# Asking for two transfers later in a fused attention and mixture-of-experts kernel

## Chip, cores and metric

The kernel runs on one core of a Trainium2 chip. The metric is the time on the device in microseconds.

## The reference

The first half is attention with one key and value head for all query heads: 8 batches, 16 heads, 384 tokens, head size 64. The second half sends each of the 3072 tokens (width 1024, the 16 heads side by side) to one of 16 experts by a gate of two levels and multiplies the expert's output by the two gate weights.

```python
scores = scale * np.matmul(q, k.transpose(0, 1, 3, 2))
scores = scores - np.max(scores, axis=-1, keepdims=True)
attn = np.exp(scores)
attn = attn / (np.sum(attn, axis=-1, keepdims=True) + 1e-09)
x = np.matmul(attn, v)              # then (B, H, S, D) -> (B*S, H*D)
...
g_idx = np.argmax(x @ w_group, axis=1)             # one of 4 groups
e_idx = np.argmax(xg @ w_expert[g], axis=1)        # one of 4 experts in it
h = np.maximum(xg[mask_e] @ w1[g, e], 0.0)
out[tok_idx] = (g_w * e_w)[:, None] * (h @ w2[g, e])
```

## The kernel before

Attention is a loop of 96 steps (`i`). Twelve steps are one batch (a "group" below), in three tiles `t` of 128 tokens with four steps each; a step handles two units of two heads by two. In a step PE makes the scores (L210), DVE their row maxima (L221) and the transposition of the probabilities of two steps before (L245), ACT the exponentials (L224), DVE the reciprocal of the sums (L235), and POOL the scaling (L239). In the first two steps of a tile PE works on the expert of an earlier batch (`main_expert`, L483 and L499) and on the gate's logits (L284); in the last two it multiplies the previous tile's probabilities by the values (`pv`, L261, 96 matmuls each).

At the end of a tile `pv_out` copies the result to `xt` and POOL casts it into `xb` (L276), the batch's tokens in bf16; there are two such buffers. The batch's most frequent expert is computed in place from `xb`. Tokens of other experts are handled after the main work by a loop over a list of (batch, expert) pairs with a count that the gate gives; that loop reads the tokens again from device memory. For this `keep_xb` (L474) copies `xb` of each batch but the last to `xb_scratch`, 768 KB in one DMA. In the profiled execution this loop has no turn.

The order of the work is written out by hand. `at(slot, where, fn, ...)` enters a call in a table, and the loop runs the table's calls of step `i` at fixed places in the step; "g" is the last of them. Each engine, SP included, works its own list of instructions in the order in which the program issues them, and waits only for the data, buffers and earlier transfers that an instruction needs.

SP's list holds, per group: the loads of queries `load_q` (L123, four DMAs of 224 KB for tiles from the sixth on; two buffers, so tile t + 2 takes that of tile t), of keys `load_k` (L133) and values `load_v` (L166, two buffers), the stores of the expert's rows y (L550), and the copy `keep_xb`. POOL issues the loads of the experts' weights (L458). The queries of a tile are reordered by DVE in two halves (`q_blocks`, L199): the first half in the second step of the tile before, the second half in the first step of the tile itself.

At the end of step 16 after the start of a batch, which is the fifth step of the next one, the table before holds the copy, the values' load and the queries' load, in this order.

Of the kernel before, what the change touches and what calls it, by code (L numbers as in the profile page):

```python
# [19 lines left out]
def kernel(  # L20
# [18 lines left out]
    ST = S // P  # L39
# [720 lines left out]
    def at(slot, where, fn, *args):  # L760
        later.setdefault((slot, where), []).append((fn, args))
# [8 lines left out]
    for b in range(B):  # L770
        s0 = SB * b
        for x, j0, j1 in ((s0 + 8, 0, 1), (s0 + 16, 1, ST)):
            at(x, "m2", logits, b, j0, j1)
            at(x + 1, "m0" if b and j0 == 0 else "v", logits_out, b, j0, j1)
        at(s0 + 9, "m0" if b else "v", gate_first, b)
        at(s0 + 9, "m3" if b else "m2", gate_choose, b)
        at(s0 + 9, "w", gate_score, b)
        at(s0 + 9, "w", gate_pick, b)
        at(s0 + (13 if b == B - 1 else 12), "w", gate_picked, b)
        if b == B - 1:  # L780
            at(s0 + 9, "w", load_main, b, 0)
            at(s0 + 10, "w", load_main, b, 1)
        else:
            at(s0 + 9, "g", load_main, b, 0)
            at(s0 + 9, "g", load_main, b, 1)
            at(s0 + 16, "g", keep_xb, b)
        at(s0 + 17, "v", gate_masks, b)
        x = s0 + 18
        at(x, "e", gate_values, b)
        at(s0 + (19 if b == B - 2 else 22), "w", gate_selected, b)  # L790
        if b == B - 1:
            at(s0 + 13, "w", gate_pick_second, b)
        if b + 1 < B:
            at(s0 + 2, "g", load_k, b + 1)
            at(s0 + 4, "g", load_v, b + 1)
            at(s0 + 7, "g", scale_k, b + 1)
            at(s0 + 8, "e", k_blocks, b + 1)
    for t in range(NT):
        for x, u, half in ((4 * t, t, 1), (4 * t + 1, t + 1, 0)):
            if u < TQ:  # L800
                at(x, "m1", q_group, u, half)
            elif u < NT:
                at(x, "e", q_blocks, u, half)
        if t < NT - 2:
            at(4 * t, "g", load_q, t + 2)

    load_k_first()
    load_q(0, first=True)
# [24 lines left out]
    for i in range(NSL):  # L833
        t, p = i // 4, i % 4
# [31 lines left out]
    b = B - 1  # L866
# [137 lines left out]
```

## Time and profile before

| what | value |
|---|---|
| median of 3 runs | 507.35 us (505.65 to 508.06) |
| profiled execution, its own time | 507.63 us |
| span of its instructions | 506.2 us |
| mean granted TensorE clock | 0.992 |
| PE, DVE, ACT, POOL busy | 94%, 82%, 63%, 58% of the span |
| moved by DMA | 83.17 MB, mean 164 GB/s |

Times in the profile are microseconds from the start of the span. In a group's line come the line of the kernel, engine, operation, output and inputs, shapes and count; in a wait's line the one that waits, what released it, then total time, how often, and the longest. An SP row of the timeline is an instruction that issues a DMA, not the transfer itself; "to landing" is the time from issue until the data is there. "PEld" is the loading of matmul weights, "issue" a time in which an engine waited for nothing that the profile shows.

### The profile page before, as it was taken

The page shows a single profiled execution, that of the slowest core. Times are in us where ns is not written, and L with a number is a line of the kernel's source. Part 1 is how long each engine was busy: PE and PEld are TensorE (multiplying, and loading weights), DVE is VectorE, ACT ScalarE, POOL GpSimd, SP SyncE. Part 2 cuts the span into 40 slices and gives each one's busy share as a digit, 9 for nine tenths or more (in the row PEclk, how much of TensorE's full clock was granted, in tenths as well). Part 3 has the DMA queues.
Part 4 walks back from the last instruction along what each step waited for, and adds up shares of the span by engine and source line. Part 5 has one row for each costly group of instructions (what it writes and reads, how often), then busy time and mean ns, then how long its engine had stood idle before and what let it go on. Part 6 is the DMA issues. An engine that isn't in the chain of part 4 may idle for free. (4 is left out here: it accounts for less than half of the span.)

```text
span 506.2 us, 20018 instructions
## 1 busy us (share of the span) xinstructions
PE 478.0 (94%) x8240; PEld 258.8 (51%) x8257; DVE 413.2 (82%) x743; ACT 319.5 (63%) x998; POOL 292.5 (58%) x532
## 2 busy tenths in 40 slices
PE   7597789999999999999999999999999999999993
PEld 3144355555455455554555455554555455555652
DVE  3889979998799888998799988998899888892550
ACT  4776756766765775766766766666666766662420
POOL 1665865585476654585466664774566754675132
PEclk9998999999999999999999999999999999999998
DMA  7612997389955999379964999379964995069993
GB/s 116 130 31 43 172 239 197 74 138 229 246 124 101 209 243 243 71 136 227 239 147 82 203 237 254 73 137 225 224 184 78 192 240 165 3 110 225 245 220 123
DMA packets 63388, 83.17 MB, mean 164 GB/s; under 512 B 20151, under 2 KB 39739, under 8 KB 63040
## 3 DMA queue, kind: packets, MB, share of 16 engines
q0 software_dynamic: 18736, 39.32, 41.9%
q1 hardware_dynamic: 43600, 42.25, 34.0%
q8 instruction: 66, 1.08, 0.9%
q10 hardware_dynamic: 960, 0.30, 0.3%
q14 instruction: 26, 0.21, 0.1%
HBM read 101.52 MB, written 18.22 MB: 237 GB/s over the span
## 5 line engine op out<-in xcount | busy, mean ns | idle before, releaser
L239 POOL TENSOR_SCALAR pr<-pr,rinv 128x384 f32<-128x384 f32 x384 | 217.3, 585 | 149.1 <-DVE rinv L235 136.1
L224 ACT ACTIVATE pr<-s,nmx 128x384 f32<-128x384 f32 x384 | 217.6, 579 | 133.2 <-DVE nmx L221 122.6
L221 DVE TENSOR_REDUCE nmx<-s 128x2 f32<-128x768 f32 x192 | 174.3, 948 | 47.5 <-PE s L210 46.4
L245 DVE STREAM_TRANSPOSE ring<-pr 128x768 f32<-128x768 f32 x192 | 175.4, 952 | 0.1
L210 PE MATMUL s<-kt,qt 64*64 64x384 f32 x1536 | 149.9, 500 | 13.7 <-ACT pr L224 12.4
L261 PE MATMUL x<-ring,v_sb 32*64 32x256 f32 x4608 | 138.4, 379 | 0.1
L261 PEld LDWEIGHTS x<-ring,v_sb 32*64 32x64 f32 x4608 | 101.9, 131 | 43.8 <-issue 23.6
L210 PEld LDWEIGHTS s<-kt,qt 64*64 64x64 f32 x1536 | 48.9, 133 | 82.9 <-ACT pr L224 43.7
L224 ACT ACTIVATION_READ_ACCUMULATOR pr<-s,nmx 128x1 f32 x384 | 77.9, 203 | 0.0
L483 PE MATMUL x<-xb,w 128*128 128x384 bf16 x448 | 76.6, 326 | 0.0
L483 PEld LDWEIGHTS <-w 128*128 128x128 bf16 x512 | 47.7, 98 | 42.2 <-issue 12.6
L499 PE MATMUL x<-w,h_t 128*128 128x512 bf16 x276 | 64.6, 380 | 0.6
L499 PEld LDWEIGHTS <-h_t 128*128 128x128 bf16 x392 | 36.4, 98 | 51.5 <-issue 12.1
L458 POOL DMA_DIRECT2D w<-in_moe_w_dram x36 | 27.4, 772 | 10.8 <-issue 8.9
L275 ACT COPY xt<-x 128x256 f32<-128x256 f32 x96 | 28.9, 387 | 3.1 <-PE x L261 3.1
L489 ACT ACTIVATE h_t<-x 128x384 bf16<-128x384 f32 x56 | 25.3, 501 | 6.5 <-PE x L483 6.5
L518 ACT ACTIVATE y<-x,gsel 128x512 f32<-128x512 f32 x36 | 24.8, 693 | 3.2 <-PE x L499 3.2
L276 POOL CAST xb<-xt 128x1024 bf16<-128x1024 f32 x24 | 24.9, 1036 | 3.2 <-ACT xt L275 3.2
L199 DVE STREAM_TRANSPOSE qt<-q_sb 128x512 f32<-128x512 f32 x38 | 26.1, 688 | 0.0
L499 PE MATMUL sb<-w,h_t 128*128 128x512 bf16 (+1 forms) x99 | 21.5, 362 | 0.3
L518 ACT ACTIVATE y<-sb,gsel 128x512 f32<-128x512 f32 (+1 forms) x10 | 6.7, 666 | 18.6 <-PE sb L499 18.6
L235 DVE RECIPROCAL rinv<-ssum 128x4 f32<-128x4 f32 x96 | 13.9, 145 | 3.2 <-ACT pr L224 3.2
(134 smaller groups left out, 157.4 us busy)
## 6 DMA issues: line engine op xcount, KB each, us to landing
w<-in_moe_w_dram POOLq DMA_DIRECT2D x36, 1024.0 KB, 13.2
q_sb<-in_q_dram SPq DMA_DIRECT2D x76, 224.0 KB, 6.0
out_dram<-y SPq DMA_DIRECT2D x84, 128.0 KB, 6.6
xb_scratch<-xb SPq DMA_DIRECT2D x7, 768.0 KB, 4.3
v_sb<-in_v_dram SPq DMA_DIRECT2D x32, 96.0 KB, 3.9
kk<-in_k_dram SPq DMA_DIRECT2D x28, 92.0 KB, 3.9
q_sb<-in_q_dram SPq DMA_DIRECT2D x16, 128.0 KB, 3.4
q_sb<-in_q_dram SPq DMA_DIRECT2D x5, 64.0 KB, 3.0
```

The source lines that it names most:

```text
L199: nc.vector.transpose(out=qt[:].rearrange("p (x d) -> p x d", d=32), in_=q_sb[:, :, 0:32])
L210: nc.tensor.matmul(out=s[m * D:(m + 1) * D, h, 0:S], lhsT=qt[r, ts(2 * cc + m, D)], rhs=kt[r, :], start=True, stop=True, tile_position=(h ...
L221: nc.vector.tensor_reduce(out=nmx[:], in_=s[:, :, 0:S], axis=AX.X, op=ALU.max, negate=True)
L224: nc.scalar.activation(out=pr[:, h, :], in_=s[:, h, 0:S], func=ACTF.Exp, bias=nmx[:, h:h + 1], scale=1.0, accum_out=ssum[:, k, h:h + 1],)
L239: nc.gpsimd.tensor_scalar(out=pr, in0=pr, scalar1=rinv[:, k, h:h + 1], scalar2=1.0, op0=ALU.mult, op1=ALU.mult)
L245: nc.vector.transpose(out=ring[:, (u // 4) % 3, u % 4].rearrange("p h s -> p (h s)"), in_=st.pop(("pr", u))[:].rearrange("p h s -> p (h s)"),)
L261: nc.tensor.matmul(out=o[i][h * D:(h + 1) * D, 0:2 * P].rearrange("d (g c q) -> d g c q", g=2, c=4), lhsT=v_sb[r, n, :], rhs=ring[r, a:z + ...
L275: nc.scalar.copy(out=xt[:, :, ts(i, 32)], in_=o[:, 0:2 * P].rearrange("p (c q) -> p c q", c=KO))
L458: nc.gpsimd.dma_start(out=w[:, o:o + 4, :], in_=views[n][ds(e, 1), :, o:o + 4, :].rearrange("o p c f -> (o p) c f"))
L483: nc.tensor.matmul(out=hp[:, 0:S], lhsT=w1[:, ko, ts(fc, P)], rhs=xb[:, ko, :], start=(ko == 0), stop=(ko == KO - 1))
L499: nc.tensor.matmul(out=yp, lhsT=h_t[:, fo, ts(j, P)], rhs=w2[:, fo, at_:at_ + w], start=(fo == 0), stop=(fo == FO - 1),)
L518: nc.scalar.activation(out=y[:, at_:at_ + w], in_=yp, func=ACTF.Copy, scale=g)
```

## The change

The copy of the tokens is entered at the end of step `s0 + 19` in place of `s0 + 16` (`s0` is the batch's first step; seven copies). For tiles with `t > 3` and `t % 3 == 1` the load of the queries of tile `t + 2` is entered at the end of step `4 * t + 2` in place of `4 * t`; these are six loads. No instruction is added or removed.

```diff
         else:
             at(s0 + 9, "g", load_main, b, 0)
             at(s0 + 9, "g", load_main, b, 1)
-            at(s0 + 16, "g", keep_xb, b)
+            at(s0 + 19, "g", keep_xb, b)
         at(s0 + 17, "v", gate_masks, b)
...
         if t < NT - 2:
-            at(4 * t, "g", load_q, t + 2)
+            at(4 * t + (2 if t > ST and t % ST == 1 else 0), "g", load_q, t + 2)
```

## The prediction

> **What bounds the kernel now.** I read the page first, then the waits of the engines, then the waits and the timeline of SP (the queue that the change edits), and last PE in the steps around the copy.
>
> ```profile
> span 506.2 us, 20018 instructions
> ...
> PE 478.0 (94%) x8240; PEld 258.8 (51%) x8257; DVE 413.2 (82%) x743; ACT 319.5 (63%) x998; POOL 292.5 (58%) x532
> ...
> q8 instruction: 66, 1.08, 0.9%
> ```
>
> PE is busy for 94% of the span. The third line counts the packets that bring instructions: 66 of them with 1.08 MB, so about 16 KB each; they matter for one rival below. The waits of the engines say who holds whom:
>
> ```profile
> POOL pr L239 <- DVE rinv L235: 136.1, 78, 9.7
> ACT pr L224 <- DVE nmx L221: 122.6, 88, 3.7
> DVE nmx L221 <- PE s L210: 46.4, 60, 2.4
> PEld s L210 <- ACT pr L224: 43.7, 79, 2.3
> ...
> PEld x L261 <- issue: 23.6, 42, 0.6
> ...
> PEld x L187 <- DMA wge<-in_moe_w_expert_dram: 0.6, 1, 0.6
> ```
>
> PE, DVE and ACT hold one another in the softmax loop. In the whole answer one line alone names a transfer for which a computing engine waits: 0.6 us for the gate's weights, once, at the start. No engine waits for queries, values or the tokens' copy. So a step of attention ends by PE and the softmax chain, not by a transfer, and what the change can win is not a wait for data. It moves transfers on SP, and SP's own waits are these:
>
> ```profile
> SPq L550 <- ACT y L518: 152.0, 10, 34.4
> SPq L123 <- DVE qt L199: 71.9, 9, 14.2
> SPq L133 <- DMA q_sb<-in_q_dram: 43.3, 20, 4.3
> ...
> SPq L474 <- POOL xb L276: 12.0, 1, 12.0
> ```
>
> SP works its list in order and mostly stands at a store of y, at a q buffer that is not yet free, or at a k load that wants earlier q loads landed. The slots of the program ("step 16", "step 18") are therefore only places in that list, not times.
>
> **Which time the copy and the q load have.** The timeline of SP in the third group of twelve steps (the last row is from a narrower window and shows the third and fourth DMA of the first q load):
>
> ```profile
> 184.24 7.46 SPq L133 DMA_DIRECT2D kk<-in_k_dram  x4
> 191.80 1.77 SPq L550 DMA_DIRECT2D out_dram<-y  x4
> 193.67 0.38 SPq L474 DMA_DIRECT2D xb_scratch<-xb  x1
> 194.14 2.63 SPq L166 DMA_DIRECT2D v_sb<-in_v_dram  x4
> 196.87 15.62 SPq L123 DMA_DIRECT2D q_sb<-in_q_dram  x8
> ...
> 197.77 0.94 SPq L123 DMA_DIRECT2D q_sb<-in_q_dram  x2
> ```
>
> And DVE, where each step has one reciprocal (L235) and the two reorderings of queries (L199) per tile:
>
> ```profile
> 188.94 0.14 DVE L235 RECIPROCAL rinv<-ssum 128x4 f32<-128x4 f32 x1
> 188.99 0.68 DVE L199 STREAM_TRANSPOSE qt<-q_sb 128x512 f32<-128x512 f32 x1
> ...
> 196.41 0.14 DVE L235 RECIPROCAL rinv<-ssum 128x4 f32<-128x4 f32 x1
> ...
> 204.66 0.14 DVE L235 RECIPROCAL rinv<-ssum 128x4 f32<-128x4 f32 x1
> ...
> 209.33 0.14 DVE L235 RECIPROCAL rinv<-ssum 128x4 f32<-128x4 f32 x1
> ...
> 210.00 0.67 DVE L199 STREAM_TRANSPOSE qt<-q_sb 128x512 f32<-128x512 f32 x1
> ...
> 215.69 0.71 DVE L199 STREAM_TRANSPOSE qt<-q_sb 128x512 f32<-128x512 f32 x1
> ```
>
> The reciprocals at 188.94, 196.41, 204.66 and 209.33 are those of steps 16, 17, 19 and 20 of the group. The q load of "step 16" needs the buffer that L199 finishes reading at 188.99 + 0.68 = 189.67. SP comes to it at 196.87, over 7 us after it is free, because it first has k, y, the copy and v to issue. So SP never waits there for step 16, and would not wait for step 18 either.
>
> **The change part by part.**
>
> *The q load put two steps later* (six loads of four DMAs). SP's list from step 16 to 20 reads y, copy, v, q, q before, and y, v, q, copy, q after. Nothing that SP waits for stands between step 16 and step 18 of the list, and the q load keeps the one condition that it had, the buffer free at 189.67. So it isn't asked for later: without the copy ahead of it, it is asked for 194.14 - 193.67 = 0.47 us earlier, at 196.4, and v at 193.7. It is first used at 215.69, about 19 us after. Price: 0. What hides it is that distance:
>
> ```profile
> L474 SPq DMA_DIRECT2D xb_scratch<-xb x7: 370/376/386, 76.0 to 422.8; - x7
> DMA to landing us min/median/max: 3.7/4.3/5.1
> ...
> DMA to landing us min/median/max: 3.0/6.0/17.2
> ```
>
> The first two lines are the copy's, the last that of the q loads of L123: at their longest, 17.2 us, a load asked for at 196.4 lands at 213.6, still before 215.69. With the cover gone DVE would stand at L199, and the next row maxima (L221) and through them ACT and PE behind it.
>
> *The copy put three steps later* (seven copies; six change places with v and q, the seventh has neither near it). It is now issued after v (2.73 us from 194.14 to 196.87) and q (197.77 + 0.94 - 196.87 = 1.84 us): 193.67 + 2.73 + 1.84 = 198.2, some 4.6 us later, in step 18 and not in step 19. Nobody reads what it writes within the timeline, and its source buffer is one of two, written again a whole group of twelve steps later. Behind it on SP stands only the second q load, which can't start before L199 ends at 210.00 + 0.67 = 210.67. Price: 0; it would cost something only if the copy took until then, over 12 us against 5.1 at most. In the first group the copy also waited 12.0 us for POOL's cast (the line of SP's waits), with v and q behind it; v need no longer stand behind that wait, and no engine waits for v. Price: 0.
>
> *What the transfers then look like.* The windows show the burst and the empty stretch (the columns end with PEclk, DMA share and GB/s):
>
> ```profile
> 193.70:198.00 4.30, 4.30 (x55) 2.19 (x61) 4.16 (x11) 2.59 (x9) 1.63 (x4) 1.00 0.97 316
> 198.00:203.50 5.50, 5.50 (x158) 3.47 (x150) 5.33 (x9) 3.63 (x13) 3.58 (x8) 1.00 0.99 188
> 203.50:210.50 7.00, 7.00 (x162) 3.96 (x150) 5.93 (x10) 5.40 (x18) 5.26 (x11) 1.00 0.03 7
> ```
>
> The engines that move data are full from 193.7 to 203.5 and empty from 203.5 to 210.5. The change issues the same DMAs, all by 198.6, so the burst keeps its length and the empty stretch stays empty; only the order inside changes, q ahead of the copy.
>
> *What PE sees of the order.* The one trace of transfers on PE that I find is in the product with the values (L261), step 19 of a group; five groups, PE's rows, and of the second the rows of the weight loads:
>
> ```profile
> 144.47 2.85 PE L261 MATMUL x<-ring,v_sb 32*64 32x256 f32 x96
> ...
> 201.68 3.29 PE L261 MATMUL x<-ring,v_sb 32*64 32x256 f32 x96
> ...
> 259.34 3.23 PE L261 MATMUL x<-ring,v_sb 32*64 32x256 f32 x96
> ...
> 316.93 3.18 PE L261 MATMUL x<-ring,v_sb 32*64 32x256 f32 x96
> ...
> 374.47 2.85 PE L261 MATMUL x<-ring,v_sb 32*64 32x256 f32 x96
> ...
> 201.68 0.62 PEld L261 LDWEIGHTS x<-ring,v_sb 32*64 32x64 f32 x18 [0.60 <-issue]
> 202.56 1.96 PEld L261 LDWEIGHTS x<-ring,v_sb 32*64 32x64 f32 x78 [0.26 <-issue]
> ```
>
> The same 96 matmuls take 2.85 us in two groups and 0.44, 0.38 and 0.33 us longer in three. Nothing releases PE there ("issue"): its list of instructions stops for a moment after the 18th weight load, while q is arriving. I read it as a block of instructions that came late among the data packets; this is inferred. In all it is 0.44 + 0.38 + 0.33 = 1.15 us. Putting the copy behind q can remove it (lower bound -1.15 us) or give one such stop to each of the seven copies (upper bound 7 x 0.44 = +3.1 us). I take 0: at 201.7 the engines that move data are full before and after.
>
> The Trainium skill ("Runtime: NRT & Kernel Launch", Instruction fetch mechanics) says that instructions come in blocks of 16 KiB over a DMA queue of their own, fetched while the engine runs the previous ones, and mostly hidden. The size agrees with the packets of the page; the 0.26 us gap is not hidden, if my reading is right. By the page the term is 0, as taken.
>
> Sum: 0 + 0 + 0 on the profiled execution's 507.63 us (span 506.2 and 1.43 around it). That one lies 0.28 us above the median of the three runs, so the forecast is the median, rounded: 507.4 us. The runs went from 505.65 to 508.06 without any change.
>
> **The rivals.** *The stops go away.* If the data packets beside q were what delayed the instructions, the three stops vanish: 507.35 - 1.15 = 506.2 us. For it: they occur only in the steps in which the burst lies. Against it: the burst is as full as before. This is still within 0.5%.
>
> *Every copy brings a stop (slower).* Place: steps 18 to 20 of a group. The copy, now at 198.2 and behind q in the queue, moves to about 201 to 204, into PE's densest lists, the product with the values at 201.68 and what follows. If each of seven copies makes PE stop once for 0.44 us, the time is 507.35 + 3.1 = 510.4 us. It decides for slower from 2.54 / 7 = 0.36 us per group. For it: three of five groups show a stop of that size now. Against it: two groups with the same burst show none, and scores and experts' matmuls leave PE's list more room than L261 does. The Trainium skill ("DMA: Bandwidth & Descriptors", Queues, rings and completion order) says that a data engine turns between queues a whole packet at a time; by that rule large packets ahead of a block of instructions hold it up longer, and this rival follows. No row here separates packets of one size from those of another.
>
> *It does what it says.* If the list does bind SP to the steps, q is asked for before the reciprocal of step 19 at 204.66 and the copy after it, at some 205 to 207, into the empty stretch. The burst gets shorter, q still lands ahead of 215.69 at its median of 6.0 us (asked for at 204, at 210), and the time is that of the first rival at best, 506.2 to 507.4 us. Against it: SP issued k, y, copy, v and q back to back.
>
> **How the numbers follow.** A measurement of this kernel can tell about 0.5%, 2.54 us, from no change. Forecast 507.4 us: 0.64. Stops gone, 506.2: 0.16. A stop per copy, 510.4: 0.13. As it says: 0.07. The range reaches from 505.3 (the lowest run is 505.65; two cases lean to that side) to 509.9 us, below the price of the slower rival, whose chance is most of what is left out. Faster by over 0.5% needs a gain of which no row shows the source, and gets 0.12 for that, from the tails of the forecast and of the two cases below it; slower gets 0.10 from the copy's rival and 0.05 from tails, 0.15; within 0.5% the rest, 0.73.
>
> **What would show it.** Right: on SP's timeline y, v, q, copy back to back, v about half a microsecond earlier, the copy 4 to 5 us later, near 198; the stretch from 203.5 to 210.5 as empty as before; no new line of a computing engine waiting for a transfer. Wrong, towards the slower rival: L261 of step 19 over 3 us in more groups than three, with gaps put down to "issue". Wrong in the premise: the copy issued after 204, or L199 waiting for a q load.

## The result and the profile after

Over 20 runs of each the change has a median of 508.49 us (505.28 to 509.66) and the kernel before 505.76 us (504.31 to 508.06). The ratio is 1.0047, 95% interval 1.0033 to 1.0061: 0.47% slower, 2.4 us by the ratio. That is within the 0.5% of the forecast's class, but the interval reaches past it. The three runs known ahead lay high; the median before is 1.6 us lower than they said. The profiled execution took 507.77 us with a span of 506.3. All ratios here leave out runs more than 1.5% above the fastest of their kernel: two of twelve in experiment 3 (704 us at a granted clock of 0.655, which stays unexplained), five of twelve in 5 and one of six in 12.

SP's timeline of the third group after:

```profile
191.03 1.77 SPq L550 DMA_DIRECT2D out_dram<-y  x4
192.90 1.76 SPq L166 DMA_DIRECT2D v_sb<-in_v_dram  x4
194.77 1.85 SPq L123 DMA_DIRECT2D q_sb<-in_q_dram  x4
196.72 0.40 SPq L474 DMA_DIRECT2D xb_scratch<-xb  x1
210.47 1.79 SPq L123 DMA_DIRECT2D q_sb<-in_q_dram  x4
```

The order is y, v, q, copy, q, back to back. Counted from the first store of y, v is asked for 0.47 us earlier than before (1.87 for 2.34), q 1.33 us earlier (3.74 for 5.07) and the copy 3.8 us later (5.69 for 1.87). Nothing comes two or three steps later. The windows, moved by the 0.8 us that this execution is ahead (columns as before, the last two DMA share and GB/s):

```profile
192.90:197.20 4.30, 4.30 (x54) 2.23 (x60) 4.20 (x10) 2.52 (x9) 1.78 (x4) 1.00 0.83 233
197.20:202.70 5.50, 4.98 (x130) 2.87 (x122) 5.32 (x9) 3.71 (x13) 3.52 (x9) 1.00 0.98 248
202.70:209.70 7.00, 7.00 (x178) 4.21 (x166) 5.21 (x9) 5.17 (x18) 4.65 (x9) 1.00 0.03 11
```

The first window is less full than before (0.83 for 0.97), the burst ends where it ended, and the empty stretch is as empty as before (0.03). What is new is in the second line: PE is busy for 4.98 of 5.50 us, where it was busy for all. The product with the values in step 19 shows where, group by group (PE's rows; where it stopped in the middle, two rows with the gap behind the second):

```profile
85.46 0.86 PE L261 MATMUL x<-ring,v_sb 32*64 32x256 f32 x17
86.74 2.42 PE L261 MATMUL x<-ring,v_sb 32*64 32x256 f32 x79 [0.42 <-issue]
...
143.52 2.85 PE L261 MATMUL x<-ring,v_sb 32*64 32x256 f32 x96
...
200.73 1.07 PE L261 MATMUL x<-ring,v_sb 32*64 32x256 f32 x18
202.33 2.41 PE L261 MATMUL x<-ring,v_sb 32*64 32x256 f32 x78 [0.52 <-issue]
...
259.10 2.85 PE L261 MATMUL x<-ring,v_sb 32*64 32x256 f32 x96
...
316.31 1.07 PE L261 MATMUL x<-ring,v_sb 32*64 32x256 f32 x19
317.67 2.41 PE L261 MATMUL x<-ring,v_sb 32*64 32x256 f32 x77 [0.29 <-issue]
...
374.45 2.85 PE L261 MATMUL x<-ring,v_sb 32*64 32x256 f32 x96
```

The third group took 202.33 + 2.41 - 200.73 = 4.01 us for what takes 2.85 without a stop. In the three groups that stop, PE loses 0.85, 1.16 and 0.92 us (from the first weight load to the last, against 2.26 us without a stop), 2.93 us in all; before it was 1.15 us. The line of the waits that holds these stops, that of L261, went from 23.6 to 25.6 us in total and from 0.6 to 1.0 us for the longest; the line of L210 hardly moved (26.9 us before):

```profile
PEld s L210 <- issue: 27.3, 151, 1.2
PEld x L261 <- issue: 25.6, 42, 1.0
```

No computing engine has a new wait for a transfer. The steps say the same, each taken from one reciprocal of DVE (L235) to the next: from step 24 of the loop to its end no step differs by more than 0.03 us between the two profiles, except step 19 of the third, fourth and fifth group (+0.72, -0.38 and +0.59 us), which are the stops. The two spans are nearly equal (506.2 and 506.3) because the profiled execution of before lost about as much in its first 24 steps; single profiles show where time is lost, the ratio says how much on average.

### The profile page after: what moved, and what is told of

Its sections match the earlier page's. It is cut to its first block, busy times and chain, and to the rows that moved or that the text cites. A ratio compares the mean times of both kernels' runs of the same rounds, so it can differ in the third digit from the quotient of the medians.

```text
span 506.3 us, 20018 instructions
## 1 busy us (share of the span) xinstructions
PE 477.1 (94%) x8240; PEld 257.4 (51%) x8257; DVE 412.9 (82%) x743; ACT 319.9 (63%) x998; POOL 293.6 (58%) x532
## 3 DMA queue, kind: packets, MB, share of 16 engines
q8 instruction: 66, 1.08, 0.9%
## 5 line engine op out<-in xcount | busy, mean ns | idle before, releaser
L210 PE MATMUL s<-kt,qt 64*64 64x384 f32 x1536 | 149.1, 497 | 13.5 <-ACT pr L224 12.4
L261 PE MATMUL x<-ring,v_sb 32*64 32x256 f32 x4608 | 138.9, 379 | 1.4 <-issue 1.2
L261 PEld LDWEIGHTS x<-ring,v_sb 32*64 32x64 f32 x4608 | 101.4, 131 | 45.6 <-issue 25.6
L210 PEld LDWEIGHTS s<-kt,qt 64*64 64x64 f32 x1536 | 48.4, 132 | 83.1 <-ACT pr L224 44.0
L235 DVE RECIPROCAL rinv<-ssum 128x4 f32<-128x4 f32 x96 | 13.9, 144 | 3.3 <-ACT pr L224 3.3
```

What stands on the lines that cost most here:

```text
L210: nc.tensor.matmul(out=s[m * D:(m + 1) * D, h, 0:S], lhsT=qt[r, ts(2 * cc + m, D)], rhs=kt[r, :], start=True, stop=True, tile_position=(h ...
L261: nc.tensor.matmul(out=o[i][h * D:(h + 1) * D, 0:2 * P].rearrange("d (g c q) -> d g c q", g=2, c=4), lhsT=v_sb[r, n, :], rhs=ring[r, a:z + ...
```

## The experiments

Ratios are to the kernel before, run on the same chip beside each, with 95% intervals.

**1. The queries' part alone.**

```diff
             at(s0 + 16, "g", keep_xb, b)
...
-            at(4 * t, "g", load_q, t + 2)
+            at(4 * t + (2 if t > ST and t % ST == 1 else 0), "g", load_q, t + 2)
```

> Only the queries' line of the change; the copy stays at step 16. If my reading of SP holds (the step of the program is only a place in SP's list, and nothing lies between the two places), this is before's list of instructions on every engine and the ratio to before is 1.000 within its interval, some 0.1 to 0.2%. If putting the load two steps later counts by itself, the ratio is near the whole change's 1.005 and SP issues the load later than before, near 205 us in the third group.

Measured 0.9991 (0.9975 to 1.0007). The list of instructions is that of before on every engine, SP included: this part of the change is nothing. It also shows how a kernel without any change varies: its trace has one stop of 0.11 us in step 19 of all groups, before's had three of 0.33 to 0.44.

```profile
PEld x L261 <- issue: 22.9, 39, 0.6
```

The whole change is therefore one of order: v and q ahead of the copy. Is it the copy behind q that costs, or q being earlier?

**2. No copy.**

```diff
-            at(s0 + 19, "g", keep_xb, b)
```

> The change without the seven copies (their scratch stays unwritten; the loop that would read it has no turn). Theory A, the copy's data behind q holds up a block of PE's instructions: the stops of L261 in step 19 fall to at most before's (1.15 us in all, against some 2.9 us after), ratio 0.995 to 1.000. Theory B, it is v and q being asked for about half a microsecond to two microseconds earlier that puts q onto the block of instructions: they are as early here, so stops of 0.9 to 1.2 us stay and the ratio is 1.004 to 1.006.

Measured 1.0013 (0.9993 to 1.0034), between the two theories. Stops stay in three groups (1.05, 0.67 and 0.38 us), but the mean is nearer to before than to the change.

```profile
PEld x L261 <- issue: 24.5, 42, 0.9
```

So the copy behind q is a good part of the cost (1.0047 against 1.0013). PE still stops here without any copy, but so it does before, and a ratio of 1.0013 can't be told from 1.

**3. The copy held to step 19.**

```diff
+    def hold(b):
+        nc.sync.dma_start(out=mark_dram[b], in_=st["rinv"][0:16, 0, 0:1])
...
+            at(s0 + 19, "g", hold, b)
             at(s0 + 19, "g", keep_xb, b)
```

> The change, with a 64-byte store of the reciprocals of step 19 ahead of each copy on SP, so that the copy can't be issued before that step: now it is asked for near 205 us in the third group, in the stretch without transfers, as the change's words have it. Theory A: no copy data meets the block of instructions that step 19 needs, stops at most before's, ratio 0.995 to 1.000, faster than the change by 0.5 to 1%. Theory B: as the change, 1.004 to 1.006.

Measured 1.0012 (0.9991 to 1.0032), the same as with no copy at all, though above what theory A gave. The copy was now really in the empty stretch, some 9 us behind q:

```profile
193.97 1.85 SPq L124 DMA_DIRECT2D q_sb<-in_q_dram  x4
202.93 0.32 SPq L476 DMA_DIRECT2D mark<-rinv  x1
203.34 0.74 SPq L479 DMA_DIRECT2D xb_scratch<-xb  x1
```

Two ways of taking the copy out of the burst give one result. Neither ratio can be told from 1, so they don't show that q being earlier costs something by itself.

**4. The copy in small rows.**

```diff
-    xb_dram = nc.dram_tensor("xb_scratch", [B, P, KO * S], BF16).ap()
+    xb_dram = nc.dram_tensor("xb_scratch", [B, P, KO, S + 32], BF16).ap()
...
-        nc.sync.dma_start(out=xb_dram[b], in_=st["xb", b][:].rearrange("p c t -> p (c t)"))
+        nc.sync.dma_start(out=xb_dram[b][:, :, 0:S], in_=st["xb", b][:])
```

> The change, with the copy's rows in the scratch padded, so that it moves pieces of 768 bytes in place of 6144 (the same bytes, eight times the packets). If it is the size of the copy's packets that holds up the instructions: stops back to before's, ratio 0.998 to 1.002. If it is only that the data engines are full for longer at this point: the copy takes longer than before (about 3 us at the rate of q), stops stay or grow, ratio 1.004 to 1.010.

Measured 1.003 (1.0003 to 1.0057): it reaches into both expectations. In its profile the instruction packet that comes between steps 18 and 19 took at most 1.29 us in any of the six groups, against 2.50 us in one group of the change. With one profile of each, whether large packets hold up the instructions more than small ones still stays open.

**5. The copy twice.**

```diff
     def keep_xb(b):
+        if b < B - 1:
+            nc.sync.dma_start(out=xb_again[b], in_=st["xb", b][:].rearrange("p c t -> p (c t)"))
         nc.sync.dma_start(out=xb_dram[b], in_=st["xb", b][:].rearrange("p c t -> p (c t)"))
```

> The change, with each copy made twice in a row (the second into a scratch of its own). If the copy's data behind q is what makes PE's block of instructions late, a burst longer by one more copy (some 2.5 to 3 us) finds the block more often: more or longer stops in step 19, ratio to before 1.006 to 1.012. If only the order of v and q counts, or if the block is caught by q alone, nothing is added: 1.003 to 1.006, as the change.

Measured 1.004 (1.0003 to 1.0077), below the figure expected and inside the other case's 1.003 to 1.006. But the twelve runs spread from 505.08 to 517.18 us, and their median is 511.67 against 506.80 us, 1.0096. The profile is of a run of 508.21 us; PE stops in step 19 of five of the six groups there, 3.1 us in all, against three groups and 2.93 us in the change. What the longest runs lost isn't shown by a profile, so I count this as support, not proof.

**6. Both transfers really later.** POOL reads a column of the old queries at step 18, so SP has to wait for that step before it loads into the buffer.

```diff
+    def still_read(t):
+        touch = pool.tile([P, 1], FP32, tag="touch", bufs=1)
+        nc.gpsimd.tensor_copy(out=touch[:], in_=st["q", t][:, 0, 0:1])
...
+        if t > ST and t % ST == 1 and t < NT - 2:
+            at(4 * t + 2, "g", still_read, t)
         if t < NT - 2:
             at(4 * t + (2 if t > ST and t % ST == 1 else 0), "g", load_q, t + 2)
```

> The change, with one read of a column of the old queries by POOL at step 18 (six reads), so that SP has to wait for step 18 before it loads into that buffer, and the copy behind it on SP comes later still: now both transfers come when the change's words say, q near 204 and the copy near 206 in the third group. Theory A, the block of instructions that PE needs in step 19 (asked for near 198 to 200) is late because of q and the copy: at that time the data engines are nearly empty, so step 19 has no stops, and the ratio is 0.994 to 0.998. Rival, stops have nothing to do with transfers: they stay as in the change, 1.003 to 1.006. Rival, the next block (near 204) is caught in its place and stops appear in step 20: 1.000 to 1.004.

Measured 0.998 (0.9959 to 1.0001), 0.67% below the change. SP's timeline and PE's line of waits (L265 is L261 of the other kernels):

```profile
194.45 1.77 SPq L170 DMA_DIRECT2D v_sb<-in_v_dram  x4
204.77 1.80 SPq L123 DMA_DIRECT2D q_sb<-in_q_dram  x4
206.62 0.45 SPq L478 DMA_DIRECT2D xb_scratch<-xb  x1
210.61 1.79 SPq L123 DMA_DIRECT2D q_sb<-in_q_dram  x4
```

```profile
PEld x L265 <- issue: 22.9, 39, 0.6
```

Step 19 has no stop in any group, and none came up in step 20. This is what the change's words describe, and it isn't slower.

**9. Only the queries really later.** The same read by POOL, with the copy at its old place ahead of v (`at(s0 + 16, "g", keep_xb, b)`).

> The kernel before, its copy at its old place ahead of v, and only the queries of every third tile made to wait for step 18 by POOL's read. Compared with the version in which q and the copy both come late. If q is what catches the block of instructions between steps 18 and 19 (stops stayed without any copy), this alone removes the stops of step 19: ratio 0.995 to 1.000, like that version's 0.998. If the copy has to be out of the way too, the ratio stays at 1.000 to 1.003 with stops in step 19.

Measured 0.9984 (0.9965 to 1.0003), as in 6, and again no stop in step 19. SP's timeline, then PE's line of waits:

```profile
191.64 0.37 SPq L478 DMA_DIRECT2D xb_scratch<-xb  x1
192.11 2.62 SPq L170 DMA_DIRECT2D v_sb<-in_v_dram  x4
202.65 8.08 SPq L123 DMA_DIRECT2D q_sb<-in_q_dram  x8
```

```profile
PEld x L265 <- issue: 23.2, 40, 0.6
```

The copy may stay where it was. In this profile it is enough that q is not under way between steps 18 and 19; the ratio alone, whose interval reaches 1.0003, doesn't show a gain over before.

**7 and 8. Other beginnings of the blocks.** In the profile before there are 66 instruction packets of 16 KB to PE's 8240 matmuls and 8257 weight loads, some 250 to a packet; what one packet brings is called a block here. 128 instructions more for PE, about half a block, in the change (7) and in the kernel before (8):

```diff
-    busy(5)
+    x = xbank()
+    for _ in range(69):
+        nc.tensor.matmul(out=x[:, 0:32], lhsT=blank[:, 0:P], rhs=blank[:, 0:32], start=True, stop=True)
     prep_first()
```

> The change, with 69 matmuls of 32 columns in place of the 5 of 512 that warm PE up at the start: 128 more instructions, half a block of 16 KB, so every later block of PE's list begins half a block earlier in the program; transfers and data as in the change; at most 1 us is added at the start. If the stops come from blocks that are fetched between steps 18 and 19, where q and the copy are under way, they go or move to other steps, and with the dense list of L261 no longer at the end of a late block the ratio to before is 0.994 to 1.001. If the transfers disturb PE in another way (its reads or writes of SBUF), the shift changes nothing: stops in step 19, 1.004 to 1.007.

> The kernel before with the same 128 instructions more at the start. By the theory of late blocks its stops in step 19 (1.15 us in the profile) go as well, and with them the difference between the two orders on SP: ratio 0.994 to 1.000, and within 0.2% of the change shifted in the same way. If the transfers disturb PE in another way: 1.000 to 1.002.

Measured 1.0274 (1.0242 to 1.0306) and 1.02 (1.017 to 1.023). The gain didn't come. In both profiles nearly all stops left step 19 (two remain in 7) and came up in steps 15 to 17 of each of the seven later groups, about 2 us a group. PE's rows of step 15 in the fourth group of 7:

```profile
240.44 1.52 PE L210 MATMUL s<-kt,qt 64*64 64x384 f32 x16
241.89 1.98 PE L261 MATMUL x<-ring,v_sb 32*64 32x256 f32 x64
244.47 1.12 PE L261 MATMUL x<-ring,v_sb 32*64 32x256 f32 x32 [0.59 <-issue]
```

That settles what the stops are. The work and the transfers of 8 are those of before and only the place in the program where each 16 KB begins was moved, and the time rose by 2%. In the traces of all fourteen kernels the weight loads of L261 stop 45 times for 0.2 us or more, and each time they go on 1.19 to 1.57 us after the end of an instruction packet. The packets ahead of L261's stops in step 15 took only 0.96 to 1.01 us, so these blocks were late by a late start. At that point the data engines are full (in the third group of 8 a share of 1.07 to 1.12 from 180 to 190 us) with the experts' weights and queries; which of the two delays the blocks was not tested.

**10 and 11. Both really later, and other shifts.** Kernel 6 with a quarter (37 matmuls of 64 columns, 64 instructions) and three quarters of a block (101 of 32 columns, 192 instructions).

> Both transfers really later, and 64 more instructions of PE at the start (37 matmuls of 64 columns in place of 5 of 512): a quarter of a block. Half a block put stops of about 2 us per group into steps 15 to 17, whatever the order on SP. If what counts is where in the program the blocks begin, a quarter of a block gives stops in other steps again: somewhere between 0.996 (none) and 1.02 (all groups), and the same step in every group. If the shift by half a block was slow only through its longer start, this is 0.998 as without the shift.

> Both transfers really later, and 192 more instructions of PE at the start (101 matmuls of 32 columns), three quarters of a block. The same theories: 0.996 to 1.02 with stops in one and the same step of every group if the beginnings of the blocks decide, 0.998 if they don't.

Measured 1.0058 (1.0037 to 1.0079) and 0.9961 (0.9942 to 0.998). With a quarter, 0.58 to 1.05 us are lost between the reciprocals of steps 15 and 16 in all seven later groups; with three quarters none after the first 24 steps, and it is the fastest kernel here, 0.4% below before.

**12. The change itself, shifted by three quarters of a block.** As 11, with q and the copy where the change has them.

> The change as it is, with q and the copy at 194 to 204 as in the change, and 192 more instructions of PE at the start. If the change costs time only because a block of PE's instructions is under way between steps 18 and 19 when q and the copy are, the cost goes with the block: ratio 0.995 to 0.998, as with both transfers really later and the same shift, and no stops in step 19. If q and the copy cost something by themselves, 0.3 to 0.5% are left on top: 0.999 to 1.002.

Measured 1.0104 (1.0054 to 1.0153), a miss: step 19 stops again, up to 2.1 us in one place. The profile is of the fastest of the six runs, 506.79 us; what the others lost isn't shown.

```profile
PEld x L261 <- issue: 25.7, 41, 2.1
```

I had thought that three quarters of a block would take the block out of the burst. It doesn't: the block is then needed later in step 19's L261, and q and the copy still delay it. In the third group of 12 its packet took an ordinary 1.01 us but started at 201.62, 1.05 us behind the first weight load of step 19's L261; the packets of q had ended at 200.45 and those of the copy went on to 203.48. In 11, with q and the copy out of the way, the packet started 3.23 us ahead of that load and took 0.93 us. 11 and 12 differ only in POOL's six reads, and with them in when SP asks for q and the copy, and they are 1.4% apart (0.9961 and 1.0104, each to before on its own chip). This is the cleanest pair on what these transfers can do to PE.

**The blocks themselves.** For the third group's block between steps 18 and 19, worked out from the instruction packets in the traces: its start after one and the same instruction of PE (a weight load of step 18's L261), how long its packet took, and what PE lost in step 19 (us).

```
kernel              start   packet   lost
before               0.77     1.39    0.44
after                0.41     2.50    1.16
1 q part alone      -0.05     1.05    0
2 no copy            0.20     1.34    0
3 copy held          1.18     1.39    0.89
4 small rows         0.42     1.20    0
```

Where start and packet sum to 1.62 or less, nothing is lost; above it (2.16, 2.91, 2.57) the loss is the sum less about 1.7. The other groups of these kernels and of 5, 6 and 9 agree, 54 blocks in all: the 35 with a sum of 1.62 or less lose nothing, and the 19 above it all lose, 18 of them the sum less 1.57 to 1.90 (one, in 5, the sum less 2.21). A block that lands later than PE's list reaches it stops PE by just that much.

A block can be late in two ways, and the change shows both. In its third group the packet was long (2.50); in its first and fifth the packet was ordinary and the start was late (1.61 + 1.08, lost 0.85, and 1.18 + 1.39, lost 0.92). In these profiles late starts come with q: with q under way (before, the change, 1 to 5) the start lay between -1.73 and 1.64, with q later (6 and 9) between -2.31 and -0.13. Packets of over 1.41 us came only with the copy in large rows right behind q, one of six in the change and four of six in 5 (1.71 to 2.83). The start varies from run to run even with the same instructions (before and 1), which is why groups stop or don't by chance and why the effect is a mean. What sets it within that spread is not shown.

## Why the prediction was right or wrong

- **No engine waits for the data that is moved**: right, before and after.
- **SP's list, not the step, sets the time**: right, and shown by 1. The order and the empty stretch came as said. The copy is 3.8 us later (4.6 forecast) and q 1.33 us earlier (0.47 forecast): the four loads of v took SP 1.76 us in place of 2.63, apparently because they no longer stand right behind the copy. In 9, with the copy ahead of v, they again took 2.62 us.
- **q and the copy priced at 0 for SP and for data**: right. They cost nothing there, though the copy now took 7.4 us to land (median) in place of 4.3.
- **What PE sees of the order, taken as 0 between -1.15 and +3.1**: this is the step that failed. It measured +2.4 us (0.47% of 505.76; in the two profiles 2.93 - 1.15 = +1.8 us). The reason given, that the data engines are full before and after, was too coarse: what delays a block is what is under way when it comes, and with the order y, v, q, copy the block started late in two groups (1.61 and 1.18 us) and its packet was long in a third (2.50 us). The mechanism stood in the text as the slower rival, a stop of 0.44 us for each of seven copies. Its place was right and its chance of 0.13 looks too small; its price of 3.1 us came near by two errors, since only three groups stopped in the profile, but for 0.85 to 1.16 us each.
- **The number, 507.4 us for a measured 508.49**: this is near by luck. The three runs it was taken from lay 1.6 us above the median before (505.76), which made up for a good part of the cost that was put at 0; from 505.76 the same working would have given 505.8, 2.7 us short.
- **"A block of instructions that came late"**: inferred then, shown now by 7, 8, 11 with 12, and the table. By the Trainium skill ("Runtime: NRT & Kernel Launch", Instruction fetch mechanics) such fetches are mostly hidden. By count the trace agrees: in the profile before, L261 stops behind four of the 66 packets. But those few cost 0.11 (experiment 1) to 2.93 us (the change) in step 19, and with unlucky beginnings of the blocks 2% and 2.7% of the time, so for this kernel they can't be put at 0.
- **The rival that data engines turn between queues by whole packets** (the Trainium skill, "DMA: Bandwidth & Descriptors", Queues, rings and completion order): not decided. The long packets of the change and of 5, and their absence in 4, fit it; the ratio of 4 is unclear, and what makes a block start late is open.
- **The rival "it does what it says"**: false of the change as written; made true in 6 it gave 0.998 (0.9959 to 1.0001), which agrees with its price, at best the first rival's 506.2 from 507.35 or 0.998.

## What to carry to other kernels

Where a list of one queue is filled by hand, the step at which a transfer is entered is only a place in that list: look for what the queue waits for ahead of it, and if the transfer has to come later, give it something to wait for. In an unrolled kernel near its PE bound, transfers that nobody waits for can still cost time, by holding up the blocks of instructions; look for idle time put down to "issue" inside a uniform run of matmuls. Where a change of order or of a few instructions moves the time by some tenths of a per cent, compare the stops step by step and over many runs, before explaining it by data.

## What was not expected of the hardware

64, 128 and 192 more instructions of PE at the start moved the time by +0.8% (1.0058 against 0.998), +2.0% (before) or +2.3% (the change), and -0.2% (0.9961 against 0.998, with q and the copy later) or +0.6% (1.0104 against 1.0047, the change): the place where the 16 KB blocks begin can matter more to this kernel than the change that was studied. The packet of such a block took 0.88 to 1.4 us in most cases, 2.50 us in the change, ahead of its longest stop, and up to 2.83 us in 5. From the second group on, four loads of values took SP 2.62 us or more to issue right behind the 768 KB copy and mostly 1.76 to 1.8 us without it; in 7, without it, four of five groups took 2.72 to 3.34 us, so the copy is not the only cause.
